# Last Y turns next to their table, moved parameter gradients, W1 turned by DMA, b2 on VectorE; three dense steps instead of two per spectrum

## The chip, the core and the metric

The kernel runs on one core of a Trainium2 chip. The core has a matrix engine (TensorE, PE in the profile, with its weight loads shown as PEld), a vector engine (VectorE, DVE), a scalar engine (ScalarE, ACT), a general engine (GpSimd, POOL) and SyncE (SP), which here only issues DMAs. Each engine takes its own instructions in order. DMAs are issued by SP, ACT or POOL and stand in the order of the issuing engine's program. The metric is the device time of one execution in microseconds.

## The reference

The forward function mixes two branches over x of 2048 positions and 448 channels (bf16), and the kernel computes its output and all the gradients for grad_out:

```python
def _A_ref(u, A_re, A_im, B_re, B_im, C_re, C_im, log_dt, Dskip):
    dt = jnp.exp(log_dt)[:, None]
    ...
    P = jnp.exp(logdA[:, :, None] * l[None, None, :])
    K = jnp.einsum("dn,dnl,dn->dl", Cc, P, dB).real          # 448 x 2048
    ...
    Yf = Uf * Kf                                             # FFTs of length 4096
    y = irfft(Yf)[:L] + u * Dskip
def _B_ref(x, w1, b1, w2, b2):
    h = jnp.einsum("bsd,df->bsf", x, w1) + b1
    r = jnp.where(h > zero, h, zero)
    return jnp.einsum("bsf,fd->bsd", r * r, w2) + b2
x = A_u
g = _sigmoid((x * gate_w).sum(-1, keepdims=True))
a = _A_ref(x, ...)          # state-space convolution, N = 256 states
b = _B_ref(x, ...)          # dense layer, F = 1792
return g * a + (1 - g) * b
...
_out, _vjp = jax.vjp(_f, ...)
_grads = _vjp(grad_out)
```

## The kernel before, in words

**The dense branch** is a generator, `dense()`. It is cut into steps, and `cost` (L907 to 910) holds a planned length for each, in tenths of a microsecond. `first_layer` runs over 14 slices j of the hidden layer: `hidden` (x times W1, ReLU into r, L651 to 666), `turn` (eight PE transposes and a squaring copy, L678 and L679), `mul_1` (the gradient of W2, L687). `second_layer` runs over the same j: `grad_h`, a `gate` on DVE, `turn`, `mul_2` (the gradient of W1), `turn_w2` and `turn_back`. `turn_w1` (L890) transposes all of W1 on PE, in 7 steps. `project` (L858) runs twice over 16 row tiles in 8 pairs n: w = 0 multiplies the squared r by W2 (branch b of the output, with b2 added by a one-row matmul, L877), w = 1 multiplies dh by the turned W1 (a gradient of x). Its row blocks are loaded three ahead by `load_rows2`. Loads and stores that are not urgent are put aside by `defer` and issued when `release` is called.

**The FFT stage** comes first. Forward transforms of u and of the gated gradient go in two stages with a trip through device memory between: `fwd1` stores to gd, `load_s1` reads it back, `fwd2` makes the spectrum. `spectra(q)` does that for two inputs in each of four quarters, `FW` says how many dense steps stand behind each of fwd2's four parts. `powers` makes powers of the state matrix between them (DVE and ACT in turn), `cmul` and `inv1` form the inverse transform for the gradient of the convolution's kernel K. Up to here the framework's scheduler orders the work; from L958 on (`manual_schedule`) the order is the one written.

**The periods.** The 448 channels are done in 14 chunks c of 32. For each c DVE builds two tables: Y (`seeds_y`, `build_y`, L991 to 994, tokens YS, Y0 to Y4) and X (`step_x`, tokens X0 to X2). `kgen` (token KM, L1055) multiplies them on PE into a part of K; `k_out` (KO) copies it out. `load_yt` (token LY, L1074) turns Y by DMA on the SP queue, four DMA transposes per c, into four ring buffers. Y has one buffer, so the seeds of the next chunk wait until the turns have read it. One period later, `back_z` (Z0 to Z3, L1099) multiplies the turned Y with the gradient of K, `back_p` (P0, P1) multiplies by X on DVE, and `back_s` (S, L1127) sums on PE into the parameter sums s_d. `PERIOD` (L1243) is the order of these tokens; each D in it stands for the dense steps that are due by cost, spread evenly so that all but the last 8 (TAILN) are done when period 13 reaches KM.

**The end, before.** Period 13: KM, KO, then `reload_k` (K read back from k_d in 16 DMAs, half on SP, half on POOL), P0 SA P1 S WD, the last 8 dense steps, `again` (copies on DVE), `fwd1` of K, LY (the last four turns, on SP), the M2 load, `load_s1` (q = 0 on POOL, the others on SP behind the turns), Z0 to P1 of chunk 13, `fwd2`. Then, for w = 0 and 1, `product` (DVE) and `inv1` (`back1`) for four quarters, with stores to hd; the loop of out_0 (L1526 to 1556: a correction matmul and inv2, L306 and L308, a DVE sum and an ACT copy per tile), the loop of out_1 (L1557 to 1569). `oq` are four buffers in Y's memory: inv1 stages its hd stores there, and both output loops put their tiles there. `param_grads` (L1387) makes the gradients of the state parameters for four blocks dt of channels, eight short steps each, mostly on DVE (L1399 is its helper); `Pg(n)` runs n steps.

The lines on which the change turns:

```python
    FW, IV = (0, 1, 0, 1), (2, 2)                                                        # L943
    period(NCH - 1, ["KM", "KO"])                                                        # L1355
    reload_k()
    period(NCH - 1, "P0 SA P1 S WD".split())
    N_(TAILN)
    ...
    K.fwd1(lambda j: xv[:, JO.index(j)], gd[2], stage=stg + ...)                         # L1457
    period(NCH - 1, ["LY"])
    G_.dma_start(M2v, cdr["M2"].ap())
    ...
    period(NCH, "Z0 Z1 Z2 P0 Z3 P1".split())                                             # L1464
```

## Time and profile before

| what | value |
|---|---|
| median of 3 runs | 830.41 us (829.63 to 832.44) |
| the profiled execution | 828.05 us |
| its span, first to last instruction | 826.3 us |
| mean granted PE clock | 0.884 |
| data moved by DMA | 181.84 MB, mean 220 GB/s |
| groups of the dense branch on PE | L687 50.7 us (x224) and more, L651 48.1 us (x168) and more, L880 37.9 us (x168) and more |
| Y table on DVE | L991, L992, L994: 48.0, 47.2, 48.1 us (x70 each) |
| turning of W1 | L896: 8.3 us of PE (x56), L897: 6.3 us of ACT (x7) |
| b2 by matmul | L877: 6.1 us (x16) |

The span is the time from the first to the last instruction that the profiler recorded. A busy time is the sum of an engine's instruction times; matmuls overlap in the pipeline, so their sum can be above what they add to the span. Each digit of a slice line is the busy share of one fortieth of the span (20.7 us) in tenths. An instruction's idle time is the gap before it on its engine, with the work that ended the gap; a gap of an engine that nothing waits for costs nothing.

### The profile page before, as it was taken

How to read it: one execution, taken by the hardware profiler on the slowest of the kernel's cores; microseconds unless marked ns; L12 is line 12 of the kernel's file. 1: busy time of each engine (PE TensorE's matmuls, PEld its weight loads, DVE VectorE, ACT ScalarE, POOL GpSimd, SP SyncE). 2: the span in 40 equal slices, each digit the busy share in tenths (PEclk: the TensorE clock that was granted, in tenths of full speed). 3: DMA queues.
4: the chain of work that ended last, by engine and by line, in shares of the span. 5: the costliest groups of instructions: out<-in, count | busy, mean ns of one | idle time of the engine just before them, and what ended most of it. 6: DMA issues, size and time to landing. Idle time of an engine off the chain costs nothing. (4 is left out here: it accounts for less than half of the span.)

```text
span 826.3 us, 20273 instructions
## 1 busy us (share of the span) xinstructions
PE 632.6 (77%) x8477; PEld 335.2 (41%) x8477; DVE 560.4 (68%) x926; ACT 521.9 (63%) x885; POOL 159.8 (19%) x272
## 2 busy tenths in 40 slices
PE   3668957879879977869999975998999823974580
PEld 1222313324445544545656653554556501531120
DVE  4785876766835865886888885496688333594574
ACT  1796876687657756466778765785554232884562
POOL 3232111111723101012011020100001330212462
PEclk9988966899989989899999996899999975997685
DMA  9967667557897999799797979878998499999972
GB/s 209 250 183 246 246 238 268 208 223 275 281 181 125 297 233 219 148 243 232 122 245 202 183 175 232 169 156 206 175 202 210 137 252 270 392 295 312 307 197 57
DMA packets 209074, 181.84 MB, mean 220 GB/s; under 512 B 131823, under 2 KB 185542, under 8 KB 208726
## 3 DMA queue, kind: packets, MB, share of 16 engines
q1 hardware_dynamic: 186854, 121.42, 60.7%
q0 software_dynamic: 13920, 38.99, 16.4%
q10 hardware_dynamic: 8208, 20.14, 6.8%
q8 instruction: 66, 1.08, 0.5%
q14 instruction: 26, 0.21, 0.1%
HBM read 85.45 MB, written 64.32 MB: 181 GB/s over the span
## 5 line engine op out<-in xcount | busy, mean ns | idle before, releaser
L1101 ACT CAST P<-psF 128x1024 bf16<-128x1024 f32 x56 | 57.2, 1021 | 29.1 <-PE psF L1099 29.0
L687 PEld LDWEIGHTS <-U 128*128 128x128 bf16 x448 | 41.5, 101 | 48.6 <-issue 19.4
L1099 PE MATMUL psF<-S,R 41*128 41x32 bf16 x1792 | 32.2, 175 | 35.4 <-DMA R<-Y 25.9
L687 PE MATMUL psN<-S,U 128*128 128x449 bf16 x224 | 50.7, 370 | 5.5 <-issue 5.5
L651 PE MATMUL psN<-S 128*128 128x512 bf16 x168 | 48.1, 409 | 7.2 <-issue 4.3
L991 DVE TENSOR_TENSOR Y<-Y,F 128x1024 bf16<-128x1024 bf16 (+3 forms) x70 | 48.0, 685 | 3.1
L994 DVE TENSOR_TENSOR Y<-Y,F 128x1024 bf16<-128x1024 bf16 (+3 forms) x70 | 48.1, 687 | 2.4
L992 DVE TENSOR_TENSOR F<-Y,F 128x1024 bf16<-128x1024 bf16 (+3 forms) x70 | 47.2, 675 | 2.4 <-ACT F L1020 2.4
L651 PEld LDWEIGHTS <-S 128*128 128x128 bf16 x336 | 30.0, 101 | 42.4 <-issue 17.2
L1099 PEld LDWEIGHTS <-R 41*128 41x128 bf16 x1792 | 27.4, 94 | 47.7 <-DMA R<-Y 28.2
L1134 POOL DMA_DIRECT2D s_d<-st x28 | 14.0, 505 | 153.0 <-ACT st L1132 147.0
L880 PEld LDWEIGHTS <-U 128*128 128x128 bf16 x308 | 28.6, 100 | 31.3 <-issue 4.8
L679 ACT ACTIVATE U<-psN 128x1024 bf16<-128x1024 bf16 x39 | 40.2, 1030 | 0.7 <-PE psN L678 0.7
L880 PE MATMUL psN<-D,U 128*128 128x448 bf16 x168 | 37.9, 375 | 2.8 <-ACT U L865 2.8
L666 ACT ACTIVATE U<-psN,b_f 128x512 bf16<-128x512 f32 x44 | 28.5, 684 | 13.4 <-PE psN L654 6.6
L651 PE MATMUL psN<-K,S 128*128 128x512 bf16 x126 | 34.6, 405 | 0.7 <-ACT R L772 0.7
L1032 DVE COPY Y<-rec 128x256 bf16<-128x256 bf16 x14 | 10.3, 733 | 35.7 <-DMA R<-Y 23.6
L1110 DVE TENSOR_TENSOR M<-P,R 128x2048 bf16<-128x2048 bf16 x14 | 17.1, 1219 | 25.4 <-ACT P L1101 25.4
L687 PE MATMUL psX<-D,U 128*128 128x448 bf16 x128 | 29.5, 366 | 4.2 <-ACT D L693 4.2
L1127 PE MATMUL psS<-ident,P 128*64 128x128 bf16 x896 | 27.9, 219 | 4.4 <-issue 4.4
L981 DVE TENSOR_TENSOR R<-R,F 128x1024 bf16<-128x1024 bf16 (+1 forms) x14 | 13.4, 959 | 21.9 <-ACT R L1012 21.5
L880 PE MATMUL psN<-S,U 128*128 128x448 bf16 x140 | 28.2, 353 | 0.0
(367 smaller groups left out, 1671.7 us busy)
## 6 DMA issues: line engine op xcount, KB each, us to landing
sp<-K ACTq DMA_DIRECT2D x8, 896.0 KB, 5.3
U<-rT_d SPq DMA_DIRECT2D x6, 896.0 KB, 5.8
hd<-Y SPq DMA_DIRECT2D x11, 448.0 KB, 6.4
rT_d<-U POOLq DMA_DIRECT2D x9, 512.0 KB, 3.8
U<-rT_d SPq DMA_DIRECT2D x9, 512.0 KB, 5.9
X<-gd SPq DMA_DIRECT2D x5, 896.0 KB, 5.3
U<-dhT_d SPq DMA_DIRECT2D x5, 896.0 KB, 6.4
R<-sp SPq DMA_DIRECT2D x5, 896.0 KB, 11.4
```

Source lines behind the costliest of these rows:

```text
L651: T_.matmul(pss[k][:], lhsT=w[:, dt], rhs=x(2 * half + k)[:, dt], start=(dt == 0), stop=False, skip_group_check=True)
L666: S.activation(r[:, 512 * lb:512 * lb + 512], pss[k][:], ACT.Relu, bias=b1_f[:, j:j + 1])
L679: S.activation(hn[j % 2][:, 8 * th:8 * th + 8, :], ps[:], f)
L687: T_.matmul(ps[:, 0:w], lhsT=hn[j % 2][:, t, :], rhs=rhs[:, t, :], start=(t == 0), stop=(t == LT - 1))
L880: T_.matmul(ps[:, 0:D], lhsT=src[:, j, P * x:P * x + P], rhs=ws[:, j, :], start=(w == 1 and j == 0), stop=(j == FT - 1))
L991: V.tensor_tensor(out=run(yb, dst, [64, X2], [d0[1], n // d0[1]], [1, d0[1]]), in0=run(yb, 0, [64, X2], *src), in1=pr, op=ALU.mult)
L992: V.tensor_tensor(out=run(vb, 0, [n, X2], [d0[1], n // d0[1]], [1, d0[1]]), in0=run(yb, 0, [64, X2], *src), in1=pi, op=ALU.mult)
L994: return V.tensor_tensor(out=hi, in0=hi, in1=run(vb, n, [2 * n, W2], [-n, 2], [1, n]), op=ALU.add)
L1099: T_.matmul(psz[:, t, 32 * b:32 * b + 32], lhsT=yt[64 * t:64 * t + NY, b, :], rhs=DKc[64 * t:64 * t + NY, c % 2, 16 * (j % 2) + b].rearran ...
L1101: S.copy(run(zbs[c, h][:, 0:1], 16 * (j % 2), [1024, 2], [64, NA], [32, 2], [1, 16]), run(psz[:, 0, 0:1], 0, [512, 2], [1, NA], [NA, 2], [ ...
L1110: V.tensor_tensor(out=run(pr[:, 0:1], 0, [32, 64], [1, 32]), in0=run(zb[:, 0:1], 0, [32, 64], [1, 32]), in1=run(xb, 32 * h, [W2, 64], [1, ...
L1127: T_.matmul(sps[64 * h:64 * h + 64, cc, r, :], lhsT=Q[h][r][:, 1024 * t + 64 * a:1024 * t + 64 * a + 64], rhs=(nident if r == 0 and t == 1 ...
```

## The change

- b2: the one-row matmul per tile goes; b2 is loaded broadcast over the partitions, and after every second tile DVE adds it to two tiles of `br[0]` (put aside until the next even tile, `gates`).
- W1: the load of w1s and `turn_w1` go; `load_w1t` turns W1 by seven DMA transposes on SP, put aside at n = 0 to 6 of project(0), and a `release` stands between the two projections.
- `FW` becomes (1, 1, 0, 1).
- The four loads of `dbt` stand ahead of period 1 instead of behind it.
- LY of chunk 13 stands ahead of its KM; Z0 to Z3 of chunk 13 behind the last dense steps, ahead of fwd1; P0 and P1 behind fwd1. The reloads of K leave SP for ACT's queue (half stays on POOL), as do two of the k_d stores. The M2 table and the grad_out rows go to Y's memory, M2 loaded ahead of fwd1; `oq` goes to where K was.
- `load_s1` alternates POOL and SP.
- Parameter gradients: blocks 0 and 1 are loaded early; eight steps stand behind fwd1, eight in the loop of product(1), six in out_0's loop, the rest, two per tile pair, in out_1's loop. `close` (the gate gradient's last lines) is done one quarter later.
- out_0's tiles have buffers of their own (`ostage`); u's rows for the last matmul come into two slots.

```diff
-    b2row = const.tile([1, D], bf16, name="b2row")
-    nc.sync.dma_start(b2row[:], B_b2.rearrange("(o d) -> o d", o=1))
...
+    b2_bc = const.tile([P, D], bf16, name="b2_bc")
+    nc.sync.dma_start(b2_bc[:], B_b2.partition_broadcast(P))
...
                 load_rows2(0)
-                G_.dma_start(w1s[:, 0:3], bass.AP(tensor=B_w1.tensor, offset=B_w1.offset, ap=[[F, P], [P * F, 3], [1, F]]))
-                G_.dma_start(w1s[0:64, 3], bass.AP(tensor=B_w1.tensor, offset=B_w1.offset + 384 * F, ap=[[F, 64], [1, F]]))
...
-                if w == 0:
-                    T_.matmul(ps[:, 0:D], lhsT=ones_r[:], rhs=b2row[:], start=True, stop=False)
...
                 S.copy(br[w][:, t], ps[:, 0:D])
+                if x == 0:
+                    gates()
+                elif w == 0:
+                    pend.append(lambda v=br[0][:, t - 1:t + 1]: V.tensor_tensor(out=v, in0=v, in1=b2_bc[:].unsqueeze(1).to_broadcast([P, 2, D]), op=ALU.add))
                 if x == 1:
...
+                    if i < HP:
+                        defer(100 + i, lambda m=i: load_w1t(m))
...
-    def turn_w1():
...
+    def load_w1t(jp):
+        nc.sync.dma_start_transpose(out=w1T[:, 2 * jp:2 * jp + 2], in_=B_w1[:, 256 * jp:256 * jp + 256])
...
-        yield from turn_w1()
         yield from project(0, w2n)
+        release()
         yield from project(1, w1T)
...
-    FW, IV = (0, 1, 0, 1), (2, 2)
+    FW, IV = (1, 1, 0, 1), (2, 2)
...
-                (G_ if c == 9 or g % 2 == 0 else nc.sync).dma_start(bass.AP(tensor=k_d, ...
+                (G_ if c == 9 or g % 2 == 0 else nc.scalar).dma_start(bass.AP(tensor=k_d, ...
...
     period(0, ["D"] * nd)
-    period(1, "SP YS Y0 D Y1 ... X2 D WD".split())
     for lb in range(4):
         nc.sync.dma_start(dbt[lb], ...)
+    period(1, "SP YS Y0 D Y1 ... X2 D WD".split())
...
-        (nc.sync if xq % 2 else G_).dma_start(xs[p0:p0 + n, j:j + m]...
+        (nc.scalar if xq % 2 else G_).dma_start(xs[p0:p0 + n, j:j + m]...
...
-    sx = {(0, 0): load_sx(0, 0, 5), (0, 1): load_sx(0, 1, 3)}
-    period(NCH - 1, ["KM", "KO"])
+    sx = {(0, 0): load_sx(0, 0, 5)}
+    period(NCH - 1, "LY KM KO P0 SA P1".split())
     reload_k()
-    period(NCH - 1, "P0 SA P1 S WD".split())
+    period(NCH - 1, "S WD".split())
     N_(TAILN)
     release()
+    for o in ("Z0", "Z1", "Z2", "Z3"):
+        token(o, NCH)
+    for q in (1, 2):
+        sx[0, q] = load_sx(0, q, q - 1)
...
-    load_raw(0, SB[:, 3584:5120], G_)
+    load_raw(0, R2[:, 12288:13824], G_)
+    load_st(0, R2[:, 13824:15872], G_)
...
-    M2v = Fx[:, 0:4096]
+    M2v = Yf[:, 0:4096]
     K.M2 = M2v
+    G_.dma_start(M2v, cdr["M2"].ap())
+    sx[0, 3] = load_sx(0, 3, 4)
...
     K.fwd1(lambda j: xv[:, JO.index(j)], gd[2], stage=...)
-    period(NCH - 1, ["LY"])
-    G_.dma_start(M2v, cdr["M2"].ap())
+    for o in ("P0", "P1"):
+        token(o, NCH)
+    sums = back_s(NCH - 1, [Qs.pop((NCH - 1, h)) for h in range(2)])
...
-        K.load_s1(gd[2], q, s1k[q], G_ if q == 0 else None)
-    sx[0, 2] = load_sx(0, 2, 4)
-    period(NCH, "Z0 Z1 Z2 P0 Z3 P1".split())
+        K.load_s1(gd[2], q, s1k[q], G_ if q % 2 == 0 else None)
+    Pg(8)
...
+    load_raw(1, SB[:, 3584:5120], G_)
+    load_st(1, SB[:, 9856:11904], G_)
...
-    oq = [Yf[:, 1792 * i:1792 * i + 1792].rearrange("p (a d) -> p a d", d=D) for i in range(4)]
+    oq = [Fx[:, 1792 * i:1792 * i + 1792].rearrange("p (a d) -> p a d", d=D) for i in range(4)]
...
+    ostage = [KW[:, 7168 + 1792 * i:8960 + 1792 * i].rearrange("p (a d) -> p a d", d=D) for i in range(4)]
...
-        Pg((2, 2, 2, 1)[q])
+        Pg((2, 2, 2, 2)[q])
...
+    def close(q):
+
+        sl = lambda a: a[:].rearrange("p (h q x) -> p q h x", h=2, q=4)[:, q]
+        V.tensor_copy(sl(dg_b), sl(dg))
+        V.tensor_tensor(out=sl(ds_b), in0=sl(dg_b), in1=sl(gp), op=ALU.mult)
+        V.tensor_copy(sl(ds32), sl(ds_b))
+        for t in (2 * q, 2 * q + 1, 2 * q + 8, 2 * q + 9):
+            S.activation(dgt[:, t], ident[:], ACT.Copy, scale=ds32[:, t:t + 1])
     for q in range(4):
         hs = hs1[q]
-        ao = oq[q]
+        ao = ostage[q]
...
+            if x == 0 and q > 0:
+                close(q - 1)
+            Pg(int(q > 0))
...
-            Pg(3)
+            Pg(2)
```

More of the change, by code (lines that the diff above doesn't have):

```diff
@@ L909 @@
         cost += [24] + [19] * (j > 0) + [24, 19] + [6] * (4 * (j in (1, 2)))
[L910 removed]
+    cost += [19, 20, 20] + [24, 22, 24, 23] * FT + [19] + [16] * 64
     done, total = 0, len(cost)
@@ L1314, in reload @@
         xq += 1
-        (nc.sync if xq % 2 else G_).dma_start(xs[p0:p0 + n, j:j + m].rearrange("p m d -> p (m d)"), bass.AP(tensor=k_d, offset=row * D, ap=[[x * D, y] for x, y in dims] + [[1, m * D]]))
+        (nc.scalar if xq % 2 else G_).dma_start(xs[p0:p0 + n, j:j + m].rearrange("p m d -> p (m d)"), bass.AP(tensor=k_d, offset=row * D, ap=[[x * D, y] for x, y in dims] + [[1, m * D]]))
     def fix(p0, step, n, j, row, st_):
@@ L1320, in fix @@
         xq += 1
-        (nc.sync if xq % 2 else G_).dma_start(xs[p0:p0 + step * (n - 1) + 1:step, j], bass.AP(tensor=k_d, offset=row * D, ap=[[st_ * D, n], [1, D]]))
+        (nc.scalar if xq % 2 else G_).dma_start(xs[p0:p0 + step * (n - 1) + 1:step, j], bass.AP(tensor=k_d, offset=row * D, ap=[[st_ * D, n], [1, D]]))
     def reload_k():
@@ L1508 @@
         product(1, q)
-        Pg((2, 2, 2, 1)[q])
+        Pg((2, 2, 2, 2)[q])
         back1(1, q)
         if q == 0:
-            hs1.append(load_hs(1, 3, 1))
+            hs1.append(load_hs(1, 3, 2))
+    load_raw(2, SB[:, 6272:7808], G_)
+    load_st(2, SB[:, 7808:9856], G_)
     for q in range(3):
-        hs2.append(load_hs(2, q, (2, 5, 3)[q]))
+        hs2.append(load_hs(2, q, (3, 5, 0)[q]))
     K.st_more = []
-    for dt in range(1, 4):
+    for dt in range(2, 4):
         obs[dt] = Pt[:, 1536 * dt - 1536:1536 * dt]
@@ L1556 @@
             G_.dma_start(dst, ao[32 * g:32 * g + 32].rearrange("p (h x) d -> p h (x d)", h=2))
+    close(3)
     for q in range(4):
@@ L1572 @@
             for t in range(LT):
-                T_.matmul(psr[0:1, 0:D], lhsT=ds_b[:, t:t + 1], rhs=Uv[:, t, :], start=(t == 0), stop=(t == LT - 1))
+                T_.matmul(psr[0:1, 0:D], lhsT=ds_b[:, t:t + 1], rhs=Uv[t // 8][:, t % 8, :], start=(t == 0), stop=(t == LT - 1))
             S.copy(row, psr[0:1, 0:D])
```

57 lines of the change are left out of this document (18 added, 39 removed).

## The prediction

> **What bounds the kernel now.** First the busy times of the engines and their slices over the span:
>
> ```profile
> PE 632.6 (77%) x8477; PEld 335.2 (41%) x8477; DVE 560.4 (68%) x926; ACT 521.9 (63%) x885; POOL 159.8 (19%) x272
> PE   3668957879879977869999975998999823974580
> DVE  4785876766835865886888885496688333594574
> ```
>
> No engine bounds the whole span. PE is at 6 to 9 in the first quarter, nearly full up to slice 32, and then has holes. So the change has to be priced by stage: A, the FFT stage (to about 223 us), B, the periods with the dense steps (to 656), C, to the first second-stage product of the last FFT (697), and D, the end. The second view is the busy time by windows, cut at the stage and at single periods (columns: window, length, busy us of PE, PEld, DVE, ACT and POOL with their counts, granted clock, DMA share, GB/s):
>
> ```profile
> 120.00:160.00 40.00, 30.68 (x163) 12.41 (x163) 26.19 (x51) 26.69 (x44) 6.71 (x10) 0.70 0.75 271
> 386.00:414.00 28.00, 28.00 (x548) 17.68 (x546) 24.44 (x35) 21.49 (x39) 2.99 (x5) 1.00 0.77 156
> 498.00:513.50 15.50, 8.47 (x67) 5.26 (x67) 7.91 (x13) 6.65 (x10) 1.32 (x2) 0.59 0.98 249
> 672.00:697.00 25.00, 2.80 (x132) 2.36 (x133) 2.45 (x2) 3.36 (x4) 0.78 (x2) 0.50 1.09 239
> 805.00:826.30 21.30, 0.37 (x2) 0.09 (x2) 8.99 (x21) 4.86 (x12) 5.58 (x11) 0.57 0.24 59
> ```
>
> A typical period (386 to 414) is PE without a gap. The FFT stage uses PE, DVE and ACT at 65 to 77% each at a clock of 0.70. The other three rows are holes: the turning of W1, the last Y turns, and the end, where only DVE works. Third, the timelines of SP, PE and ACT in the last two holes, and the chain that ended last (columns: start, length, engine, line, instruction, in brackets the idle time before it and what ended it):
>
> ```profile
> 672.41 21.41 SPq L1074 DMA_TRANSPOSE R<-Y  x4
> 694.25 0.36 SPq L243 DMA_DIRECT2D K<-gd  x1
> 684.27 0.61 PE L1099 MATMUL psF<-S,R 41*128 41x32 bf16 x32 [15.64 <-DMA R<-Y]
> 761.59 1.16 ACT L1538 ACTIVATE Y<-psN,g 128x448 bf16<-128x448 f32 x2 [8.49 <-DMA hd<-Y]
> 764.67 0.53 PE L306 MATMUL psF<-K,nident 128*128 128x448 bf16 x1 [11.37 <-ACT Y L1538]
> 807.25 0.70 DVE Y L1399
> 814.32 0.18 DVE dlog_b L1578
> ```
>
> After fwd1 the SP queue spends 21.41 us on four Y turns; PE waits for the first 15.64 us, and the loads of the FFT's second stage stand behind them until 694.25. At 753 ACT may not write out_0's tiles, since their buffers (oq) are still being stored to hd. The chain that ended last is the parameter gradients on DVE.
>
> **The change part by part.** The sum is made against the profiled execution, 828.05 us (span 826.3); the median of the runs shown is 830.41, 2.36 above it.
>
> *A: eight more dense steps.* FW = (1,1,0,1) gives one step more in each of 8 spectra. Counted through the list of costs, 43 steps are done before the periods now, and 51 then: two more values of j in first_layer. From the FFT stage's timeline, on PE: a half of hidden takes 1.73 us (89.99 to 91.72), its turn 0.55, a mul_1 half 1.62; twice each is 7.8 per j, 15.6 for two. On ACT: 4 x 0.687 (L666), 2 x 1.03 (L679) and 0.54 (L693) per j, 10.7 for two. PE is busy 90 of 116 us between 84 and 200. Bounds: nothing, if its idle 26 us take the steps; 17, if all of it and some ACT is added. The stage is a web of short DVE-ACT-PE waits, so I take 70%: **+11**.
>
> *B: what leaves the periods.* Those 15.6 us of PE leave, one step of nine per second-layer period. But the shortest period (Y seeds at 442.2 to the next at 468.9) is 26.7 us: 12 of table building on DVE, 12.7 of four transposes, and 2 of wait; and Y has one buffer. A full period of 28 can fall only so far: about 1.2 us in seven periods and 1.6 in the first two. I take −10 (bounds −4, where that ring rules, and −15.6).
> W1: 56 transposes and seven 0.91 us copies (L896, L897) alternate on one PSUM bank from 499.26 to 513.58, 14.3 us. Seven DMA turns replace them on the SP queue. The same shape is in the trace at the start (A_re and the others, 448x256): 1.27 to 4.10 us of SP each, landing in 4.1 to 7.5. They are issued with the loads of rT at n = 0 to 6, and by the counted steps the last is released in period 11 ahead of that period's Y turns, more than 10 us before project(1) reads it. But the turning also covered the load of the second rT block: ACT waited 6.7 us for rT in all; with the cover gone I give back 5. So −9 (bounds 0, −14); the 1.3 MB load of w1s goes too.
> b2: 16 one-row matmuls, each 0.29 us until the next matmul begins (530.94 to 531.23), leave PE: 3 to 4.6, I take −3. Eight DVE adds of 128x896 at 0.625 us (row of L1539) come, 5.0 us, under a full PE (DVE 22.7 of 28 in 540 to 568); without that cover +5. The b2 broadcast load is one like dsk_bc's, on SP before fwd1.
> load_u (four 448 KB loads, 13.9 us to landing) now stands right ahead of the Y turns of period 2, which took 23.25 us against 11 to 13 in quiet periods; it comes after those of period 1, and the four dbt loads move one period forward on SP with nothing late behind them. Bounds 0 and −9 (DVE's wait there); I take −3. **B: −25**.
>
> *C: the last turns.* Counted from the last kgen (639.7). Now: dense work ends at +16.4, fwd1 +19 to +31, SP's four turns +33 to +54, fwd2 at +56.9. Then: the turns go out at about 0, beside the k_d stores and reloads. Four Z (1.7 us each with the copy, 694.32 to 696.03) come ahead of fwd1 on PE: +23. The k reload's eight DMAs leave SP for ACT: they wait for the k_d stores till 650.3 and end near 655.5, by SP's own row now. Behind them on ACT stand four project copies, whose four banks are all free, and the Z copies; PE would wait about 1 us. fwd1 23 to 35; its last stores land 8.3 later (1.7 + 6.6), the first s1 load 7.5 after that: fwd2 at about +51. P0, P1 (4.9 us) and eight Pg steps (7.2 us DVE) lie in this gap; should they be late, they are in fwd2's way by some 2 us. On POOL, load_st(0) and the M2 load (0.77 and 0.56 us) now stand ahead of fwd1's gd stores, behind the six load_raw DMAs that ended at 663.2: free at 664.6, when the first store is due at about 664.2. M2 waits there for the table to be read (+2 to +24); if the turns are late, the gd stores on POOL are late with it, which is part of the upper bound below. fwd2(0), 8.4 us long now with P0/P1 in between, gains about 1. **−7** (bounds +6, if the four turns take 21 us beside the reload and hold up Z and so fwd1; −12).
>
> A rule of the Trainium skill speaks against moving the reload: "DMA: Bandwidth & Descriptors", "Issuing engines are not separate DMA queues", says that all issuers share the same 16 engines and only the sequencer's time is saved. The trace has both: the load that POOL issued went out at 683.39, eleven us ahead of SP's, but the M2 load took 10.3 us beside the turns. By the rule alone C would be about 0, and the sum 7 higher.
>
> *D: the end.* ostage takes oq's place as the tile to be stored: ACT's 8.49 us go. Next late would be the loads of hd[2]: issued at 764.18, 6.5 to 8.8 to landing (11 with contention, 775), needed then at 779, so 4 us are left. Parameter gradients: 24.07 us of DVE in L1399, of which 17.9 lie after 787.5. Eight steps move ahead of fwd2, eight stay under product(1), six go in out_0's loop (DVE 11.67 of 23.5 busy), and ten into out_1's loop (PE 17.15 of 17.5). Then the end is PE's last product at 804.8 and its copies, 1.1 us, and not DVE's 814.3: 8.4. The six in out_0's loop, 4.5 us of DVE, and close() in another order give back about 3. **−14** (bounds −8, −18). What follows the last issue, 815.9 to 826.3, stays.
>
> Sum: 11 − 25 − 7 − 14 = −35: 828.05 − 35 = 793.05, and 2.36 more for the median: **795 us**.
>
> **The rivals.**
> *The Y ring paces the periods.* DVE waited 23.6 us for R<-Y in the periods, 11.7 of it while W1 was turned: then the W1 and dense-step gains fall from 19 to 4, **810**. Against it: only four of 12 periods show such a wait.
> *The FFT stage takes the steps for nothing.* Its clock is 0.81 (84 to 120) and 0.70 against 1.00 in full periods; 57.5 us of PE there would be 43 at full clock, 14 less, about what is added: A is 0, **784**. The Trainium skill, "TensorE: Matmul & The Clock Gate", "Part 1: The HAM clock gate", has such a rule: sustained activity opens the clock. Against it: PE's idle gaps there wait for ACT and DVE.
> *The turns and the k reload collide*, so the change doesn't bring fwd2 forward: C is +6, **808**. For it: the turns in quiet periods took 11 to 13, with large loads beside them 19 to 23.
> *Slower: W1's DMA turns hold up the Y turns.* Both stand on SP, one after the other. At the tail's price, 21.41/4 = 5.35 each, all seven in the ring's way cost 37.5: −35 + 37.5, **833**. It decides from about 5 us each. Against it: 1.3 us in five of the six rows at the start, and they come after a period's Y turns, when DVE has 11 us of P and X to do.
>
> **How the numbers follow.** Forecast 0.43 (own range 787 to 803), Y ring 0.22, steps for nothing 0.15, collision 0.12, slower 0.08. The range reaches from below 784 to above 810: 775 to 817. What a measurement of this kernel can tell from no change is about 0.3%. The first four cases are faster; of the last, 0.06 is slower and 0.02 the same.
>
> **What would show it.** Right: the four last Y turns start near the last kgen and fwd2 about 51 us after it; no L896; ACT without a wait for hd before out_0; the last DVE gradient before the last product; LY of period 2 near 12 us. Wrong: the first Y turn (now at 223.1) later by 15 or more; periods of 28 that stay at 28; DVE waiting for R<-Y in most of them; fwd1 starting 25 us or more after the last kgen.

## The result and the profile after

The changed kernel takes 801.58 us (median of 4 runs, 799.57 to 806.06) beside 830.97 us before (4 runs, 829.63 to 832.44): a ratio of 0.9653, interval 0.9604 to 0.9703. That is 29.4 us less; 35 were forecast. The profiled executions have spans of 826.3 and 804.3 us, 22.0 apart, the one of after being the longest of its four runs. The profiled execution of the first experiment's kernel ran at a mean granted clock of 0.561 and is left out, so that this kernel has a time and no stages.

The busy times and slices of the kernel after:

```profile
PE 618.2 (77%) x8366; PEld 329.4 (41%) x8405; DVE 566.3 (70%) x934; ACT 515.2 (64%) x878; POOL 160.3 (20%) x272
...
PE   3577957788897758997999986979899851587554
...
DVE  4786597576780729788989897768888445669472
```

PE has 14.4 us less of recorded work. Its weight loads are 72 fewer, as many as the 56 transposes and the 16 one-row matmuls that went; of its matmuls 111 fewer are on record, so some 39 records are missing. Its share is 77% as before: the span shrank with it. The digits 5, 1 and 5 (us 643 to 704) are the hole of the last turns, still there. The busy time by windows of the kernel after, with the columns of before, for the FFT stage and one late period:

```profile
120.00:160.00 40.00, 30.27 (x169) 11.99 (x168) 25.20 (x50) 27.94 (x49) 6.72 (x11) 0.80 0.73 259
536.20:562.70 26.50, 26.25 (x501) 16.20 (x502) 23.64 (x35) 21.31 (x25) 2.03 (x4) 0.94 1.12 212
```

In 120 to 160 the granted clock is 0.80 where it was 0.70, with PE as busy as before. A late period, 26.5 us, has PE busy for 26.25 of them: it is full, but shorter than 28. The same view in the stretch from the last Y turn to fwd2:

```profile
642.50:657.20 14.70, 6.47 (x151) 3.97 (x149) 4.67 (x11) 4.78 (x7) 6.63 (x13) 0.83 0.54 126
657.20:676.00 18.80, 10.09 (x41) 3.80 (x33) 8.01 (x13) 7.49 (x14) 5.50 (x9) 0.68 1.00 343
676.00:684.00 8.00, 0.00 (x0) 0.00 (x0) 7.83 (x10) 4.16 (x8) 1.01 (x2) 0.50 0.57 149
684.00:693.20 9.20, 0.02 (x2) 0.05 (x3) 4.26 (x10) 0.00 (x0) 3.92 (x8) 0.50 1.00 389
```

This is the hole that the change was to close. It is 50.7 us long; DMA moves 126 GB/s in its first 14.7 us, then is saturated for 18.8 us, then half idle, then saturated for 9.2 us more. The timeline of the kernel after in the same stretch, SP, ACT, PE and POOL:

```profile
627.34 15.20 SPq L1067 DMA_TRANSPOSE R<-Y  x4
...
646.84 3.58 ACTq L1307 DMA_DIRECT2D F<-k_d  x5
...
650.46 1.84 ACT L877 CAST D<-psN 128x448 bf16<-128x448 f32 x4 [17.68 <-DMA F<-k_d]
...
653.27 0.61 PE L1092 MATMUL psF<-S,R 41*128 41x32 bf16 x32 [6.03 <-ACT P L1094]
...
653.81 3.64 SPq L1337 DMA_DIRECT2D R<-sp  x2
...
657.50 0.42 SPq L1337 DMA_DIRECT2D U<-sp  x1
...
657.75 0.54 POOL L1455 DMA_DIRECT2D Y<-c_M  x1
...
659.65 5.08 SPq L237 DMA_DIRECT2D gd<-X  x4
...
673.94 0.90 PE L232 MATMUL psN<-F,cb_F1BD 128*128 128x448 bf16 x2 [7.06 <-ACT X L206]
...
683.14 0.33 SPq L243 DMA_DIRECT2D K<-gd  x1
...
683.62 0.56 POOL L243 DMA_DIRECT2D K<-gd  x1 [5.38 <-DMA gd<-X]
...
693.18 0.96 PE L253 MATMUL psN<-K,Y 128*64 128x448 bf16 x4 [18.33 <-DMA K<-gd]
```

The turns start with the last kgen, as expected, and last 15.20 us. ACT stands 17.68 us behind the waiting reload, so Z1 waits 6.03. The last five loads of the reload leave ACT by 650.42, 23.0 us after the first matmul of the last kgen; in the kernel before the same five left SP by 655.47, 15.8 us after it:

```profile
653.31 2.16 SPq L1315 DMA_DIRECT2D F<-k_d  x5
```

Then, in the kernel after, three loads of s/p rows and M2 go out right ahead of the stores of fwd1 (L237), fwd1 stands 7.06 us for a staging buffer, and in the last 18.33 us before fwd2 PE waits for the load of K, issued on POOL at 683.62. Landing times there (the DMA view of the kernel after, from 600 to 720; KB each, median us from issue to landing):

```profile
R<-sp SPq DMA_DIRECT2D x5, 896.0 KB, 11.8
U<-sp SPq DMA_DIRECT2D x3, 896.0 KB, 8.2
...
gd<-X SPq DMA_DIRECT2D x6, 224.0 KB, 13.6
gd<-X POOLq DMA_DIRECT2D x6, 224.0 KB, 9.3
...
K<-gd SPq DMA_DIRECT2D x1, 896.0 KB, 4.7
...
K<-gd POOLq DMA_DIRECT2D x1, 896.0 KB, 9.4
```

The stores of X landed in 6.6 and 6.7 us before. The end, first ACT's first tile of out_0, then the last instructions:

```profile
746.39 1.23 ACT L1548 ACTIVATE K<-psN,g 128x448 bf16<-128x448 f32 x2 [0.28 <-DVE X L1547]
```

```profile
789.35 0.07 DVE L1431 DVE_READ_ACCUMULATOR Y<-Y,dtc,R 64x1 f32 x1
...
791.74 0.35 PE L306 MATMUL psN<-gw_bc,X 128*128 128x448 bf16 x1
```

The wait of 8.49 us for hd is gone, and the last DVE gradient (789.35) comes ahead of the last product (791.74).

Five stages of all profiled executions, from one mark to the next, in us. Marks: the first Y turn, the last matmul of the last kgen (1.8 us behind its first, from which the prediction and the expectations of experiments 1 to 3 count; the later ones count from the last), the first matmul of fwd1, that of fwd2, the end of the span.

| kernel | to first Y turn | periods | kgen to fwd1 | fwd1 to fwd2 | fwd2 to end | ratio of times to before |
|---|---|---|---|---|---|---|
| before | 223.1 | 418.4 | 17.2 | 37.9 | 129.7 | 1 |
| after | 232.3 | 396.9 | 28.0 | 36.0 | 111.1 | 0.965 (0.960 to 0.970) |
| 1 s/p loads late | | | | | | 0.960 (0.955 to 0.964) |
| 2 reload on SP | 229.8 | 390.2 | 25.2 | 35.1 | 111.1 | 0.959 (0.955 to 0.964) |
| 3 last turns as before | 230.7 | 402.2 | 19.6 | 37.6 | 120.5 | 0.969 (0.965 to 0.974) |
| 4 W1 on PE | 230.5 | 413.3 | 26.6 | 35.5 | 112.5 | 0.985 (0.981 to 0.989) |
| 5 1 and 2 together | 230.6 | 397.2 | 23.3 | 33.2 | 116.8 | 0.964 (0.960 to 0.968) |
| 6 5, M2 first on POOL | 231.5 | 399.6 | 25.7 | 31.2 | 114.6 | 0.964 (0.961 to 0.968) |
| 7 two dense steps | 222.5 | 410.1 | 25.5 | 36.1 | 111.9 | 0.973 (0.968 to 0.978) |
| 8 out_0 in oq | 228.6 | 393.3 | 24.7 | 35.2 | 119.1 | 0.970 (0.966 to 0.974) |
| 9 gradients late | 232.8 | 394.0 | 25.0 | 34.7 | 114.4 | 0.969 (0.964 to 0.973) |
| 10 s1 loads swapped | 232.7 | 395.1 | 25.6 | 30.3 | 114.3 | 0.957 (0.952 to 0.963) |
| 11 10, early loads | 230.4 | 395.6 | 28.2 | 23.9 | 113.9 | 0.956 (0.950 to 0.962) |
| 12 11, reload on SP | 231.9 | 392.8 | 26.7 | 27.2 | 114.1 | 0.958 (0.955 to 0.961) |

The last stage in four parts, in us. Marks: the first matmul of fwd2, the first of output 0's loop, the first product with gw_bc (output 1), the last product, the end of the span.

| kernel | fwd2 to output 0 | output 0 | output 1 | last product to end |
|---|---|---|---|---|
| before | 54.9 | 36.3 | 16.7 | 21.8 |
| after | 51.8 | 30.4 | 16.7 | 12.3 |
| 3 last turns as before | 61.2 | 30.5 | 16.7 | 12.3 |
| 8 out_0 in oq | 51.5 | 38.6 | 16.7 | 12.3 |
| 9 gradients late | 51.3 | 30.8 | 17.3 | 15.0 |

Where a stage's code is that of the changed kernel, it repeats within these bounds: first turn 228.6 to 232.8 (11 profiles, mean 231.1), periods 390.2 to 402.2 (10, mean 395.7), kgen to fwd2 59.7 to 64.0 (after, 4, 7, 8 and 9, mean 61.5), fwd2 to end 111.1 to 112.5 (after, 2, 4 and 7, mean 111.7). A difference of a stage counts below where it goes beyond these. The intervals of the ratios are 3 to 5 us to each side, so most single edits are read from the stages.

### The profile page after: what moved, and what is told of

It is laid out like the page before. It is cut to its first block, busy times and chain, and to the rows that moved or that the text cites. A ratio compares the mean times of both kernels' runs of the same rounds, so it can differ in the third digit from the quotient of the medians.

```text
span 804.3 us, 20084 instructions
## 1 busy us (share of the span) xinstructions
PE 618.2 (77%) x8366; PEld 329.4 (41%) x8405; DVE 566.3 (70%) x934; ACT 515.2 (64%) x878; POOL 160.3 (20%) x272
## 3 DMA queue, kind: packets, MB, share of 16 engines
q0 software_dynamic: 14096, 39.35, 16.5%
## 4 chain that ended last, share of the span: by engine, by line
PE 32%; DMA 22%; DVE 18%; ACT 13%; issue 10%; POOL 2%; ACTq 1%; DVEq 0%; POOLq 0%; SPq 0%
PE psN L874 6%; DMA R<-Y 4%; PE psN L649 4%; PE psN L685 3%; PE psX L1048 3%; PE psS L1120 3%; DMA gd<-X 3%; DVE Y L984 2%; DVE Y L987 2%; DVE F L985 2%; DMA k_d<-X 2%; PE psF L1092 2%; PE psX L685 2%; DMA U<-rT_d 1%; DMA S<-in_B_w_dram 1%
## 5 line engine op out<-in xcount | busy, mean ns | idle before, releaser
L1092 PE MATMUL psF<-S,R 41*128 41x32 bf16 x1792 | 32.3, 176 | 29.0 <-DVE S L1078 14.8
L685 PE MATMUL psX<-D,U 128*128 128x448 bf16 x160 | 38.2, 377 | 3.6 <-ACT D L691 3.6
L664 ACT ACTIVATE U<-psN,b_f 128x512 bf16<-128x512 f32 x48 | 31.5, 685 | 13.9 <-DVE st L533 6.4
L649 PE MATMUL psN<-K,S 128*128 128x512 bf16 x100 | 29.7, 416 | 10.4 <-ACT R L770 6.1
L677 ACT ACTIVATE U<-psN 128x1024 bf16<-128x1024 bf16 x35 | 35.9, 1026 | 2.7 <-PE psN L676 2.7
L877 ACT CAST D<-psN 128x448 bf16<-128x448 f32 x16 | 8.2, 537 | 34.6 <-DMA F<-k_d 17.7
L1120 PE MATMUL psS<-ident,P 128*64 128x128 bf16 x896 | 27.9, 219 | 1.2 <-issue 1.1
L232 PEld LDWEIGHTS <-cb_F1BD 128*128 128x128 bf16 x96 | 10.6, 117 | 43.8 <-issue 40.3
## 6 DMA issues: line engine op xcount, KB each, us to landing
R<-sp SPq DMA_DIRECT2D x5, 896.0 KB, 11.8
```

Source lines behind the costliest of these rows:

```text
L649: T_.matmul(pss[k][:], lhsT=w[:, dt], rhs=x(2 * half + k)[:, dt], start=(dt == 0), stop=False, skip_group_check=True)
L664: S.activation(r[:, 512 * lb:512 * lb + 512], pss[k][:], ACT.Relu, bias=b1_f[:, j:j + 1])
L677: S.activation(hn[j % 2][:, 8 * th:8 * th + 8, :], ps[:], f)
L685: T_.matmul(ps[:, 0:w], lhsT=hn[j % 2][:, t, :], rhs=rhs[:, t, :], start=(t == 0), stop=(t == LT - 1))
L1092: T_.matmul(psz[:, t, 32 * b:32 * b + 32], lhsT=yt[64 * t:64 * t + NY, b, :], rhs=DKc[64 * t:64 * t + NY, c % 2, 16 * (j % 2) + b].rearran ...
L1120: T_.matmul(sps[64 * h:64 * h + 64, cc, r, :], lhsT=Q[h][r][:, 1024 * t + 64 * a:1024 * t + 64 * a + 64], rhs=(nident if r == 0 and t == 1 ...
```

## The experiments

**1. The s/p loads behind the stores.** Of the four loads of s/p rows ahead of fwd2 the last three are issued behind the loads of fwd1's results.

```diff
-    for q in (1, 2):
-        sx[0, q] = load_sx(0, q, q - 1)
...
-    sx[0, 3] = load_sx(0, 3, 4)
...
         K.load_s1(gd[2], q, s1k[q], G_ if q % 2 == 0 else None)
+    for q, k in ((1, 0), (2, 1), (3, 4)):
+        sx[0, q] = load_sx(0, q, k)
```

> Three of the four loads of s/p rows (sx 0,1 to 0,3, 2.7 MB together) are issued after the first-layer transform's last load instead of ahead of its stores. Theory (these loads stand ahead of the stores of fwd1 and are why a 224 KB store lands in 9 to 15 us instead of 7): the landing of gd<-X falls back to about 7 us, fwd1 loses its stall of 7 us on the staging buffers, fwd2 starts 8 to 12 us earlier (55 to 58 us after the last kgen in place of 65.8), the whole about 790 to 794 us. Rival 1 (the stores are slow because they start before the turns' other traffic ends, whatever the loads do): landings stay above 9 us, time within 3 us of the changed kernel. Rival 2 (the loads are needed at once by the products): fwd2 starts earlier, but the first product waits for its load, and the time stays at 800.

Ratio 0.960 beside 0.965: 4.6 us less, and the two intervals overlap. Undecided by itself; experiment 5 has the stages.

**2. The reload on SP.**

```diff
-        (nc.scalar if xq % 2 else G_).dma_start(xs[p0:p0 + n, j:j + m]...
+        (nc.sync if xq % 2 else G_).dma_start(xs[p0:p0 + n, j:j + m]...
```

(and the same in `fix`.)

> The reload of the kernel table's rows is issued on SP instead of on ACT, as it was before the change. Theory (ACT stands behind the waiting reload for 17.7 us, so the copies of the last turns, Z1 and with it fwd1 come 6 us late): Z0 to Z3 follow one another without the wait of 6 us for ACT, fwd1 starts 24 to 26 us after the last kgen in place of 29.9, time down by 3 to 6 us. Rival (the reload then stands behind the last Y turn on SP, and fwd1 waits for the k rows themselves): the copies into the table finish at or after where they did (24.3 us after the last kgen), fwd1 starts as late or later, time the same or up 2 to 6 us.

Z0 to Z3 then follow one another at 1.7 us without the wait for ACT, but fwd1 starts 25.2 us after the last kgen, inside the 24.7 to 28.2 of the seven kernels that have the reload on ACT. The wait is real and hardly on the path: fwd1 also needs the table, which is complete at 643.6 here, when fwd1 starts at 645.2. In the profiled execution the lower total comes from the periods (390.2), which this edit doesn't touch.

**3. The last turns where they were.** LY of chunk 13 behind fwd1, Z and P behind the loads of s1, reload and k stores on SP, M2 and G in their old memory. The three s/p loads go behind the loads of s1 (one ahead of Z and P, two behind them; the kernel before had its second ahead of period 13's KM). The rest stays changed, the eight steps of gradients ahead of fwd2 among it.

```diff
-    period(NCH - 1, "LY KM KO P0 SA P1".split())
+    period(NCH - 1, "KM KO P0 SA P1".split())
...
-    for o in ("Z0", "Z1", "Z2", "Z3"):
-        token(o, NCH)
...
+    period(NCH - 1, ["LY"])
...
+    period(NCH, "Z0 Z1 Z2 P0 Z3 P1".split())
```

> The order of the last turns is put back: the last Y turn after fwd1, Z and P after the loads of s1, reload and k stores on SP, M2 and G rows in the buffers of before, the loads of s/p rows where they were; the dense steps, W1 and b2 stay changed. By the recorded sum (the move is worth 7 us): time up by 7, about 808 us. By the two traces (fwd2 starts 65.8 us after the last kgen in place of 56.9): fwd2 starts 55 to 58 us after the last kgen, some 9 us earlier. How much of that is left at the end tells what the later part of the program got from the move: if all of the 18.6 us gained behind fwd2 belongs to other edits, time falls to about 793; if the part behind fwd2 gives back as much (DVE and ACT are busy again with Z and P there), time stays near 802; if it gives back more, over 805.

fwd2 starts 57.2 us after the last kgen, 4.3 earlier than the mean with the turns moved; but the stretch behind it is 8.8 longer. The timeline of this kernel:

```profile
666.47 20.56 SPq L1067 DMA_TRANSPOSE R<-Y  x4
...
690.07 0.96 PE L253 MATMUL psN<-K,F 128*64 128x448 bf16 x4
...
693.62 0.68 DVE L1393 TENSOR_TENSOR Y<-D,R 128x512 f32<-128x512 f32 x1
...
696.75 0.58 PE L253 MATMUL psN<-K,F 128*64 128x448 bf16 x2 [3.81 <-ACT K L206]
...
701.31 0.58 PE L253 MATMUL psN<-K,F 128*64 128x448 bf16 x2 [3.98 <-DVE K L207]
```

The four turns run beside the stores and loads and take 20.56 us, but fwd1 itself has no stall. What it pays comes later: P1 and eight steps of gradients are on DVE from 691 to 700, and fwd2's matmuls wait 3.81 and 3.98 us for their copies. The last matmul of its first two quarters starts at 704.9, 14.8 us after the first, against 5.0 in the kernel after (693.2 to 698.2). So the move is worth 4.5 us (120.5 + 57.2 against 111.7 + 61.5), and all of it is had behind fwd2's start. But it isn't worth that alone: in the kernel before, which has no gradient steps there, the same two quarters take 7.8 us. Without the steps the move would cost 1.5 us by these rows (57.2 + 7.8 against 61.5 + 5.0, an estimate); it pays because it makes room for them. A second thing shows here: DVE's copies into the table that the reload fills end 13.8 us after the last kgen, and 15.7 in the kernel before, but 20.2 to 26.7 in the eleven profiles whose turns run beside the reload.

**4. W1 turned on PE.** `turn_w1` with its 56 transposes and seven copies is back, with the load of W1 for it; `load_w1t` goes.

```diff
-                    if i < HP:
-                        defer(100 + i, lambda m=i: load_w1t(m))
...
+        yield from turn_w1()
         yield from project(0, w2n)
-        release()
```

> W1 is turned by TensorE and copied by ACT again, as before the change, instead of by seven DMA turns on SP (26.5 us of SP in the trace). By the recorded sum (9 us, between 0 and 14): the period in which the turns stand grows by some 9 us and the time goes to about 811. By the trace (the period with the turn shrank by 7.7 us, the next grew by 1.4): up 5 to 7 us, 807 to 809. Rival (the DMA turns cost the periods as much as they save): within 3 us of the changed kernel.

The periods are 17.6 us longer than the mean and the time is 16.5 us above that of the changed kernel (0.985 - 0.965 of 831 us). The transposes of this kernel, by line (duration in ns, first and last start, then idle time in us):

```profile
L896 PE MATMUL psN<-ident,K x56: 199/230/314, 488.1 to 505.5; 128*128 128x128 bf16 x42, 64*128 64x64 bf16 x14
...
  ACT S L897: 5.8, 5
```

They and the copies alternate on one bank, as in the trace of before, over 19.4 us (487.3 to 506.7), of which 4.8 are other work. The DMA turns of the kernel after, on SP, by its timeline:

```profile
512.17 4.14 SPq L891 DMA_TRANSPOSE S<-in_B_w_dram  x1
516.40 15.32 SPq L1067 DMA_TRANSPOSE R<-Y  x4
531.82 0.52 SPq L850 DMA_DIRECT2D U<-rT_d  x1
```

They took 2.96 to 4.86 us of SP each, 26.5 in all. The one at 512.17 stands ahead of the Y turns of its period, the load of rT behind them goes out at 531.82, and this period is 36.3 us long (34.9 before). The next two are 26.5 and 27.9.

**5. Experiments 1 and 2 together.**

> The two edits together: the reload on SP, and three loads of s/p rows after the first-layer transform's last load instead of ahead of its stores. Theory (the loads, 2.7 MB, stand ahead of the stores): with the reload on SP alone the first-layer transform began 25.2 us after the last kgen, stood 5.8 us for a staging buffer, and fwd2 began 60.3 us after the last kgen; with the loads gone the stores land in 7 to 9 us, the stall is 0 to 2 us, fwd2 comes 50 to 54 us after the last kgen, and the time falls to 784 to 790 us. Rival (the M2 load, 1 MB on POOL ahead of POOL's stores, and the raw rows are enough to hold the stores up, or the stores hold themselves up): landings stay at 10 us or more, fwd2 at 57 to 61 us, time as with the reload alone, some 797.

The rival holds. The stall of fwd1 in this kernel, and the landing times from 600 to 720:

```profile
665.96 0.91 PE L232 MATMUL psN<-F,cb_F1BD 128*128 128x448 bf16 x2 [5.40 <-ACT X L206]
```

```profile
R<-sp SPq DMA_DIRECT2D x5, 896.0 KB, 20.7
U<-sp SPq DMA_DIRECT2D x3, 896.0 KB, 14.5
...
gd<-X SPq DMA_DIRECT2D x6, 224.0 KB, 5.9
gd<-X POOLq DMA_DIRECT2D x6, 224.0 KB, 9.0
...
gd<-st SPq DMA_DIRECT2D x2, 224.0 KB, 11.2
```

The 5.9 us of SP's stores are a median of four landings, the others not being on record; its two stores of st, issued in the middle of fwd1, land in 11.2 us, and POOL's in 9.0. fwd1 still waits 5.40 us for a buffer, where the seven profiles with all loads ahead show 5.50 to 7.06: the stall hardly moved. fwd1 to fwd2 gains some 2 us (33.2 against 34.7 to 36.1), and the stretch behind fwd2 loses 5 (116.8): the s/p rows land in 20.7 and 14.5 us instead of 11.8 and 8.2, when the products want them. The loads were taken out of one way and put into another.

**6. M2 ahead of the raw rows.** As 5, with M2's load ahead of `load_raw(0)` on POOL.

```diff
+    G_.dma_start(Yf[:, 0:4096], cdr["M2"].ap())
     load_raw(0, R2[:, 12288:13824], G_)
...
-    G_.dma_start(M2v, cdr["M2"].ap())
```

> As the kernel with both edits, and the M2 load (1 MB) is issued some microseconds earlier on POOL, ahead of the raw rows of the parameter gradients. Theory (what stands ahead of the stores sets when they land): POOL's stores land in 7 instead of 9 to 10 us, fwd2 another 1 to 3 us earlier, time 782 to 788. Rival (the loads of s/p rows alone were the cause, M2 costs nothing): the same time as the kernel with both edits, within 2 us.

The stall is 2.9 us, POOL's stores land in 6.5, and fwd1 to fwd2 is 2 us shorter than in 5. M2 went out 0.2 us ahead of fwd1's start, where it was 4.7 us behind it in 5, and no earlier since POOL stood behind its part of the reload. But fwd1 starts 2.4 us later here, and fwd2 comes no earlier after the last kgen (56.9 us against 56.5). Whether M2's place or the later start shortens the stall isn't told apart by this run, and the 1 to 3 us that the theory gave fwd2 didn't come. The total is that of 5.

**7. Two dense steps again.** `FW` is (0, 1, 0, 1).

> Two dense steps per spectrum again in the FFT stage, the eight steps back in the periods. By the recorded sum (11 us taken there, 10 given in the periods): first Y turn at about 220 to 222 instead of 230 to 232, the periods together 8 to 12 us longer, time within 3 us of the changed kernel. Rival 1 (the steps fill PE in periods that it paces, and cost more there than the sum says): periods longer by 13 to 16 us, time up 4 to 7. Rival 2 (they lie in the shadow of the seeds in the periods): periods longer by under 5, time down 4 to 6.

The first turn comes 8.6 us earlier, the periods are 14.4 us longer: rival 1. The first three periods, from the first seeds of Y to the fourth, take 108.7 us, and 108.8 to 114.5 with three steps (112.8 in the kernel after), so nothing comes back there; 15 come back from the fourth on. The Y turns of period 2 take 24.60 us again, with the dbt loads where the change put them. The third step is worth about 6 us net, and the time (0.973) is 6.4 us above the changed kernel's.

**8. out_0 in oq.** `ao = oq[q]` in place of `ao = ostage[q]`.

> Output 0 is staged in the buffers that the first inverse layers use (oq) instead of buffers of its own. By the recorded sum ACT's wait of 8.49 us for the hd stores ahead of output 0 returns: time up by 8 to 9 us, 810 to 812, with an ACT wait for hd of 7 to 9 us there. Rival (the wait was hidden behind the inverse layers' own loads, which end last there): the wait returns on ACT, but the time stays within 3 us.

ACT's wait is back:

```profile
742.48 1.16 ACT L1548 ACTIVATE F<-psN,g 128x448 bf16<-128x448 f32 x2 [7.51 <-DMA hd<-F]
```

The stretch behind fwd2 is 7.4 us longer than the mean, and the loop of output 0 8.2 us longer than in the kernel after, as the sum had it; the time is 4.1 us above the changed kernel's by the ratios (0.970 against 0.965).

**9. The gradients late.** `Pg(8)` behind fwd1 goes, `Pg(2)` in the loop of output 1 becomes `Pg(3)`. The rows of block 0 have been overwritten by then, so the values of outputs 2 to 8 change; the instructions are the same.

> The first eight steps of the parameter gradients don't run while the first-layer transform's spectra travel, but three at a time in the loop of output 1, at the end. By the recorded sum (DVE's tail at the end, 8.4 us, less what is given back in the loops) they come back as a tail: fwd2 starts where it did, the stretch from fwd2 to the end grows by 4 to 8 us from 111.1 us, with DVE as the last engine. Rival (the end is set by DMA and TensorE, and DVE has room there): the stretch stays within 2 us of 111, time within 2 us of the changed kernel.

The stretch behind fwd2 is 2.7 us longer, and all of that lies behind the last product (15.0 us against 12.3):

```profile
785.80 0.37 PE L308 MATMUL psN<-M,cb_Etw 128*32 128x448 bf16 x4
...
789.19 0.22 PE L1587 MATMUL psN<-ident,dlog_b 128*4 128x128 bf16 x1 [3.02 <-DVE dlog_b L1585]
```

The theory holds in kind, with less than its 4 to 8 us: DVE has a tail again. PE is done with the last product at 786.2 and waits 3.02 us for the sum of the gradients, and the chain that ended last runs over DVE, as in the kernel before. From the last gradient to the end it is 12.0 us in both (788.9 to 800.9, 814.3 to 826.3). In the kernel after the last gradient ends ahead of the last product. DVE had room for most of the eight steps in the last loop, but not for all.

**10. The s1 loads swapped.** `G_ if q % 2 else None` in place of `G_ if q % 2 == 0 else None`.

> Of the four loads of the first layer's result, 896 KB each, the first and third are issued on SP and the others on POOL, instead of the other way round. Theory (fwd2 waits for the first one alone, which on POOL takes 9.0 to 9.4 us and beside it the second, on SP, 4.7): fwd2 starts 4 to 5 us earlier against the start of the first-layer transform (31 to 32 us in place of 35 to 36), and the stretch behind it grows by 0 to 3. Rival (all four share the transfer engines, so the first lands at 9 us on SP too): no change within 1 us.

fwd1 to fwd2 is 30.3 us against 34.7 to 36.1, so the first load does land in 4.7 us on SP; the stretch behind grows by 2.6, of which 1.67 us are a wait of fwd2 for the second, now on POOL.

**11. Early loads.** With the swap; raw rows, s rows and M2 go on SP behind the last turn, ahead of the s/p loads.

```diff
-    for q in (1, 2):
-        sx[0, q] = load_sx(0, q, q - 1)
...
-    load_raw(0, R2[:, 12288:13824], G_)
-    load_st(0, R2[:, 13824:15872], G_)
+    load_raw(0, R2[:, 12288:13824], nc.sync)
+    load_st(0, R2[:, 13824:15872], nc.sync)
+    nc.sync.dma_start(Yf[:, 0:4096], cdr["M2"].ap())
+    for q in (1, 2):
+        sx[0, q] = load_sx(0, q, q - 1)
...
-    G_.dma_start(M2v, cdr["M2"].ap())
```

> As the kernel with the swapped loads; and the raw rows (0.9 MB) and M2 (1 MB) go on SP behind the last Y turn, in the stretch where the transfer engines were busy 0.45 to 0.48 of the time, instead of on POOL ahead of the first-layer stores. Theory (the stores wait behind bytes, 1.9 MB at 370 GB/s is 5 us, and those loads can be taken out of their way without making anything later): the stall of 5 to 7 us on staging buffers in the first-layer transform falls to 0 to 2, fwd2 starts 26 to 28 us after the transform's start with the swap, the stretch behind it stays at 111 to 114, time 790 to 795. Rival (the three loads of s/p rows alone hold the stores, or moving bytes only moves the wait as it did when those were late): the stall stays at 5 us or the stretch behind fwd2 grows by as much, time at 797 or more.

The same three views of this kernel, from the last Y turn on (landing times from 600 to 720):

```profile
640.00:654.20 14.20, 5.83 (x148) 3.67 (x147) 4.58 (x11) 4.78 (x7) 2.74 (x6) 0.74 0.98 266
654.20:664.50 10.30, 8.69 (x35) 3.37 (x32) 7.81 (x12) 7.37 (x13) 4.01 (x7) 0.86 0.97 337
```

```profile
gd<-X SPq DMA_DIRECT2D x6, 224.0 KB, 6.4
gd<-X POOLq DMA_DIRECT2D x6, 224.0 KB, 6.1
```

```profile
650.20 0.61 PE L1092 MATMUL psF<-S,R 41*128 41x32 bf16 x32 [6.17 <-ACT P L1094]
...
663.77 0.54 PE L232 MATMUL psN<-F,cb_F1BD 128*128 128x448 bf16 x2 [0.46 <-ACT X L206]
...
678.13 0.96 PE L253 MATMUL psN<-K,Y 128*64 128x448 bf16 x4 [13.81 <-DMA K<-gd]
```

The 14 us behind the last turn now carry 266 GB/s. The stores land in 6.4 and 6.1 us, fwd1 waits 0.46 us where it waited 7.06, and fwd2 starts 23.9 us after fwd1: 12.1 less than in the kernel after, 5.7 by the swap and 6.4 by the early loads. Behind fwd2 nothing is lost against experiment 10 (113.9, 114.3). The theory holds in its stage. Counted from the last kgen, fwd2 comes after 52.1 us against 55.9 in experiment 10: 3.8 of the 6.4 us are left, since fwd1 started 2.6 us later, which is inside the spread of that start. The totals of 10 and 11 can't be told apart (0.957, 0.956). The time is 795.8 us, 0.956 of before; its interval and that of the changed kernel overlap in 0.960 to 0.962.

**12. Early loads, reload on SP.** As 11, the reload on SP, the raw and s rows on POOL ahead of the reload.

> As the kernel with early loads, and the reload of the table's rows is on SP, the raw rows go on POOL before the reload (POOL stands 5.5 us there for the k stores), M2 on SP behind the reload. Theory (ACT stood 17.85 us behind the reload in the kernel with early loads, and Z1 waited 6.17 us for it): no wait of Z1 for ACT, fwd1 starts 23 to 25.5 us after the last kgen in place of 28.2, the transform to fwd2 stays at 24 to 26 us, fwd2 48 to 51 us after the last kgen, time 1 to 4 us below the kernel with early loads, 791 to 795. Rival (fwd1 then waits for the table's rows or the last Y turn, and M2, issued later, is back ahead of the stores): fwd1 at 25 us or later, or 28 us and more from fwd1 to fwd2; time the same or up to 3 us more.

The rival holds: Z goes through, and fwd1 then waits for the table itself.

```profile
651.41 1.65 PE L232 MATMUL psN<-F,cb_F1BD 128*128 128x448 bf16 x4 [3.70 <-DVE F L1448]
```

fwd1 starts 26.7 us after the last kgen, M2 goes out 2 us ahead of fwd1 instead of 9, with the s/p loads behind it, SP's stores of X land in 11.3 us, and fwd1 has a stall of 6.27 us again. fwd1 to fwd2 takes 27.2. The kernel is no better than 11. Both beat the kernel before and, by the stages, the changed one.

## Why the prediction came out as it did

The mark that failed is fwd2: "fwd2 at about +51". It came at +65.8, and C cost time where it was to bring 7. One sign of being wrong came with it: fwd1 started 29.9 us after the last kgen, where "25 us or more" was named. The other marks came as forecast. The sum by stages (means over profiles against the one of before): A +8.0 where +11 was taken, B -22.7 where -25, C +6.4 where -7, D -18.0 where -14. Together -26.3 against -35, by the runs -29.4. The time lies inside the forecast's own range because C is one term of four and D paid part of it back, and because B's sum came out, in part by luck.

**A, +11: right, a little high.** The first turn moved by 8.0, and back by 8.6 in experiment 7. That is about half of the 15.6 us of added PE work, where 70% was taken. The granted clock in 120 to 160 is 0.80 and 0.79 with three steps (after, experiment 4) and 0.70 with two (before, experiment 7), so the mechanism of the rival that the stage takes the steps for nothing is there. That it is what saved 3 of the 11 us isn't shown: PE's idle time can have taken them as well. The Trainium skill, "TensorE: Matmul & The Clock Gate", "Part 1: The HAM clock gate", has sustained activity open the clock. The rows of 120 to 160 agree with it.

**B, -25: near in sum, not in its terms.** Four kernels make a table of the periods: 418.4 us before, 413.3 with the dense steps but without W1's DMA turns (experiment 4), 410.1 with the DMA turns but without the dense steps (experiment 7), 395.7 with both; b2 and the dbt loads are changed in all but the first. So the dense steps, "I take −10", bring at most 5.1 alone and 14.4 beside the DMA turns; W1, "−9", brings at most 8.3 alone and 17.6 beside the steps. The sum added the two as if each were worth the same without the other. Why they are worth more together no run shows. W1's turning itself was priced rightly at 14.3 (14.6 in experiment 4), and against the 5 "given back" for the cover of the rT load ACT's wait for rT rose from 6.7 to 9.6. The note that a period could fall only to 26.7 was near the truth (one of the kernel before took 26.4 already, and most are now 26 to 28), but there were longer ones to shorten. The Y ring didn't pace them: DVE's seeds waited 8.5 us for R<-Y in all, 23.6 before. The DMA turns do cost 3 to 4.9 us of SP each and one period of 36.3, but not the 5 us in the way of the ring that the slower rival needed. b2 (-3) was not tried alone. For the loads (-3) the runs show no gain: the turns of period 2 took 11.46 us instead of 23.25, yet period 1 grew by 9.0 us in its place, where PE waits for the start of the second layer. In experiment 7, which keeps the new place of the dbt loads, the turns of period 2 took 24.60 and the first three periods were no longer. So that sign came true by the shift of the dense steps, and brought nothing.

**C, -7: wrong.** The step that failed is "fwd1 23 to 35", at both ends. fwd1 began at +29.9: the reload was to "end near 655.5, by SP's own row now", that is at +15.8, and ended at +23.0 beside the turns, ACT stood behind it, and the "about 1 us" that PE was to wait for ACT was 6.03. Experiment 2 took that wait away, and fwd1 began little earlier, since the table itself was late. And fwd1 took 20.1 us to its last copy (677.3) where the sum had 12, with its stall of 7.06 on staging buffers. These are 6.9 and 8.1 us, together the 15 by which +51 was missed. The rest, stores and first load, took 15.9 where the sum had 8.3 and 7.5.

The sum counted M2, the rows and the s/p loads as time of POOL's and SP's queues, half a microsecond each, and not as bytes: 2.7 + 1.0 + 0.9 MB, 13 us of transfer at the 343 GB/s of the saturated window, issued right ahead of the stores. With all of these issued earlier the stall is 0.46 (experiment 11). With the rows and M2 going out beside the first stores, and the s/p loads behind the stores, it is 5.40 (experiment 5). With the rows earlier, and M2 and the s/p loads in the last 2 us ahead of fwd1, it is 6.27 (experiment 12). So moving one part was not enough, in one profile each.

The move pays 4.5 us all the same, by what the sum didn't count on: it makes room for eight gradient steps ahead of fwd2 (experiment 3). The "gains about 1" of fwd2's first quarters without P0 and P1 are 2.8 (7.8 us before, 5.0 after). What the sum took as given could have been better: the first quarter of the result came by POOL in 9.4 us beside SP's 4.7, and fwd2 comes 4.4 to 5.8 us sooner after fwd1 when SP issues it (experiment 10).

The collision rival named the right sign and nearly the size (+6, 808). Half of its mechanism is there: the turns took 15.2 us, not 21, but the reload beside them was 7 us late. The other half, the stores that were held up, it doesn't have. The Trainium skill's rule of "DMA: Bandwidth & Descriptors", "Issuing engines are not separate DMA queues", has all issuers share the same engines, and by it C was 0. The runs agree where the reload changes between ACT and SP, which made no difference beyond the spread, while the same bytes put into another time took 6.4 us off fwd1 to fwd2. They disagree where SP and POOL change places: some 5 us of fwd2's start hung on which of them issued the first load.

**D, -14: right, term by term.** By the table of four parts the loop of output 0 is 5.9 us shorter, where 8.49 for the hd wait less some 3 given back were taken. Experiment 8 brings 8.2 of it back and is then 2.3 longer than before, which is what the steps and `close` in that loop cost. Behind the last product 9.5 us went, where 8.4 were taken for DVE's tail; with the eight early steps put back to the end (experiment 9) DVE ends last again, by 2.7. The 3.1 that are left lie between fwd2 and output 0, and are the quarters without P0 and P1 that the sum had put into C.

## What to carry to other kernels

Where a step is moved, count the bytes that it and its neighbours put ahead of the transfers on the path, at the rate measured there, and not only the issue time on their queues. A transfer that is merely pushed back is asked for later; look for a stretch in which DMA is half idle, and put it there. And read each stage of several profiles, since the totals of edits worth under 5 us can't be told apart here. Two edits to one stage may be worth more together than the two alone, as the dense steps and W1 were here, so undo each and not only add them up.

## What the hardware showed that was not expected

- Of two loads of 896 KB issued within 0.7 us of each other, with two more behind, the one on SP landed in 4.4 to 4.9 us and the one on POOL in 9.0 to 9.4, whichever quarter they carried (after and experiments 2 and 4 to 12). SP's went out first each time, by 0.3 us or more; but in experiment 12 POOL's first went out 0.1 us ahead of SP's second and landed 1.1 us behind it.
- A DMA that waits on ACT's queue holds ACT's compute: 17.68 us in the kernel after, 17.85 in experiment 11.
- Beside four Y turns the reload of the table was late: DVE's copies from it ended 20.2 to 26.7 us after the last kgen in eleven profiles, and 13.8 and 15.7 in the two whose turns come later (experiment 3, before).
- DMA turns of 448x256 took 2.96 to 4.86 us of SP each among a period's traffic; at the start of the kernel before, five of six rows show 1.3.
